# Attention over 512 heads: value loads and stores cut into three partition ranges

## The chip, the cores and the metric

The kernel runs on one core of a Trainium2 chip. The metric is the device time of one execution in microseconds (us); lower is better. Three timed runs of the kernel before took 1209.46, 1211.04 and 1211.22 us, median 1211.04.

The engines are named as in the profile: PE is TensorE (matrix products; PEld is its weight load), DVE is VectorE, ACT is ScalarE, POOL is GpSimd, SP is SyncE, whose queue issues every DMA of this kernel. Sixteen DMA engines carry out the transfers.

## The reference

q has the shape (16, 32, 192, 128), k and v (16, 32, 1024, 128), all in bf16. For each of the 16 x 32 = 512 heads:

```
scale  = 128 ** -0.5
scores = einsum("bhqd,bhkd->bhqk", q, k) * scale
p      = softmax(scores, axis=-1)
out    = einsum("bhqk,bhkd->bhqd", p, v)
```

So 192 queries of a head meet 1024 keys. Keys and values are 134.22 MB each, queries and results 25.17 MB each.

## The kernel before, in words

The 512 heads are worked off in 32 groups of G = 16 heads. Each group has 8 pairs of heads; a pair has 2 x 192 = 384 query rows, cut into three units of 128 rows. So a group has 24 units, and the program 768.

A unit goes through stages that stand some units apart (LAGS): PE multiplies queries and keys into `s_ps` (`qk`); DVE scales, copies to `ss` and takes the extreme value of a row (L335); ACT takes the exponential (L391), or POOL only subtracts the extreme value (L210) and the exponential comes later; PE transposes the 128 x 1024 result in eight pieces (`tr`, into `pt_ps`); ACT copies it to SBUF (L402, L404); PE multiplies it by the values (`pv`, into `o_ps`); DVE divides by the sum of the row and writes `ob` (L362, L365). Where POOL prepared the unit, `pv` also multiplies by a column of ones to get the row sums.

The inputs of a group are double-buffered: `kt`, `qt` and `vs` have NS = 2 slots, and group g uses slot g % 2. `ob` has two slots too (NSO = 2). All transfers are issued by SP, in one order written out by hand:

- At the start the first group comes in three pieces (FIRST, 2, 6 and 8 heads), each with its own semaphores (`sf`, `sfv`); then group 1 in whole by `loads(1)`.
- Then for each group g: `loads(g + 2)`, followed by `stores(g)`.
- `loads(g)` waits until PE has done the last `qk` of group g - 2 (`s_qk`), issues the keys as a DMA transpose (`kt`, L144) and the queries as a DMA transpose (`qt`, L148), waits until PE has done the last `pv` of group g - 2 (`s_pv`), and issues the values as one plain DMA of 4096 KB (`vs`, L155). In the values, partition p holds the keys 8p to 8p + 7 of every head, so one partition of one head is a run of 2 KB.
- `stores(g)` waits for DVE (`s_on`) and writes the group's results as one DMA of 768 KB (L173): 128 partitions with 24 rows of 256 B each. The last group is stored in four pieces (LAST).

Every DMA adds 16 to its semaphore when it has landed, in sixteen steps of one. PE waits for the keys (`sxk`), the queries (`sxq`) and the values (`svl`, L311) of a group at the first unit of that group; the counts come from `load_cnt(g)`, which counts 16 for each earlier use of the slot. DVE waits for the store of group g - 2 before it writes the first pair of group g into the same slot of `ob` (`store_cnt`), and SP waits for all stores at the end.

PE's order in each step is `qk` of the next unit, `pv` of the unit 8 back, `tr` of the unit 4 back; it is one queue in that order, so a wait of one of them holds up the others.

Of the kernel before, what the change touches and what calls it, by code (L numbers as in the profile page):

```python
# [13 lines left out]


def _attention_kernel(nc, q, k, v, out, G=16, NS=2, LAGS=(2, 4, 5, 8), ROUTES=(R_W, R_W, R_EA, R_W, R_EA, R_EA),
                      FIRST=((0, 2), (2, 8), (8, 16)), LAST=((0, 4), (4, 6), (6, 7), (7, 8))):
    B, H, SQ, D = q.shape
    SK = k.shape[2]
    assert D == 128 and SK == 1024 and SQ == 192, (D, SK, SQ)  # L20
# [6 lines left out]
    KT_TILES = SK // 128  # L27
# [7 lines left out]
    NSO = 2  # L35
# [4 lines left out]
    vf = v.rearrange("b h s d -> (b h) s d")  # L40
    of = out.rearrange("b h s d -> (b h) s d")

    def route(u):
        return ROUTES[u % len(ROUTES)]
# [4 lines left out]
    for u in range(NU):  # L49
        r = route(u)  # L50
# [13 lines left out]
    with ExitStack() as es:  # L64
        def sb(name, shape, dt):
            return es.enter_context(nc.sbuf_tensor(name, shape, dt))
# [4 lines left out]
        def sem(name):  # L71
            return es.enter_context(nc.semaphore(name))
# [3 lines left out]
        vs = sb("vs", [128, NS, G, KT_TILES, 128], BF16)  # L76
        ob = sb("ob", [128, NSO, PPG, 3, 128], BF16)
# [14 lines left out]
        svl = [sem("svl%d" % i) for i in range(NS)]  # L92
        sf = [sem("sf%d" % i) for i in range(len(FIRST))]
        sfv = [sem("sfv%d" % i) for i in range(len(FIRST))]
        sst = [sem("sst%d" % i) for i in range(NSO)]
# [13 lines left out]
        def unit_info(u):  # L109
            pr = u // 3  # L110
            k3 = u % 3
            g = pr // PPG
            pg = pr % PPG
            return pr, k3, g, pg
# [6 lines left out]
        def load_cnt(g):  # L121
            return 16 * (g // NS + 1 - (g % NS == 0))

        def store_cnt(g):
            return 16 * (g // NSO + 1)

        def wait_x(eng, u):
            if route(u) == R_W:
# [4 lines left out]
        def wait_evac(eng, u):  # L133
            if route(u) == R_ED:
                eng.wait_ge(s_evd, ev_cnt[u])
            else:
                eng.wait_ge(s_eva, ev_cnt[u])

        @block.sync
        def _(e):  # L140
            def load_kq(g, a, b, sems):
                s = g % NS
                h0 = g * G
                e.dma_start_transpose(  # L144
                    kt[:, s, :, a * 128:b * 128],
                    kf[h0 + a:h0 + b].rearrange("g (p t) d -> (g p) (t d)", t=KT_TILES),
                ).then_inc(sems[0], 16)
                e.dma_start_transpose(  # L148
                    qt[:, s, a * SQ:b * SQ],
                    qf[h0 + a:h0 + b].rearrange("g r d -> (g r) d"),  # L150
                ).then_inc(sems[1], 16)

            def load_v(g, a, b, sm):
                h0 = g * G
                e.dma_start(  # L155
                    vs[:, g % NS, a:b],
                    vf[h0 + a:h0 + b].rearrange("g (p t) d -> p g t d", t=KT_TILES),
                ).then_inc(sm, 16)

            def loads(g):  # L160
                s = g % NS
                last_u = (g - NS + 1) * UPG - 1
                if g >= NS:
                    e.wait_ge(s_qk, last_u + 1)
                load_kq(g, 0, G, (sxk[s], sxq[s]))
                if g >= NS:
                    e.wait_ge(s_pv, last_u + 1)
                load_v(g, 0, G, svl[s])

            def stores(g, a, b):  # L170
                so = g % NSO
                e.wait_ge(s_on, g * PPG + b)
                e.dma_start(  # L173
                    of[g * G + 2 * a:g * G + 2 * b].rearrange("h r d -> (h r) d").rearrange(
                        "(n p) d -> p n d", p=128),
                    ob[:, so, a:b].rearrange("p pg y d -> p (pg y) d"),
                ).then_inc(sst[so], 16)

            n = len(FIRST)
            for i in range(n):  # L180
                load_kq(0, *FIRST[i], (sf[i], sf[i]))
                if i > 0:
                    for i2 in range(i if i > 1 else 0, i + 1):
                        load_v(0, *FIRST[i2], sfv[i2])
            for g in range(1, min(NS, NGR)):
                loads(g)
            for g in range(NGR):
                if g + NS < NGR:
                    loads(g + NS)
                for a, b in (LAST if g == NGR - 1 else ((0, PPG),)):  # L190
                    stores(g, a, b)
            for so in range(min(NSO, NGR)):
                n_uses = len(range(so, NGR, NSO))
                if so == (NGR - 1) % NSO:
                    n_uses += len(LAST) - 1
                e.wait_ge(sst[so], 16 * n_uses)

        @block.gpsimd
        def _(gp):
# [20 lines left out]
        def _(pe):  # L220
            def product(o, w, x, at=(0, 0), start=True, stop=True, transpose=False):

                return pe.add_instruction(mybir.InstMatmult(  # L223
                    name=nc.get_next_instruction_name(),
                    engine=mybir.EngineType.PE,
                    ins=[pe.lower_ap(x), pe.lower_ap(w)],
                    outs=[pe.lower_ap(o)],
                    start_tensor_calc=start,
                    stop_tensor_calc=stop,
                    is_transpose=transpose or None,  # L230
                    tile_size=(128, w.shape[-1]),
                    tile_position=at,
                    bass_skip_group_check=True,
                    ldweights=False,
                ))

            def qk(u):
# [13 lines left out]
                if g == 0:  # L251
                    for i, (h, _) in enumerate(FIRST):
                        if u == 3 * h // 2:
                            pe.wait_ge(sf[i], 32)
                elif u % UPG == 0:
                    pe.wait_ge(sxq[s], load_cnt(g))
# [27 lines left out]
            def pv(u):  # L284
                pr, k3, g, pg = unit_info(u)
                s = g % NS
                O = o_ps[pr % 2]
                PTS = pt_sb[:, u % NPT]
                sl = O_SLOT[k3]
                a = 2 * pg  # L290
                b = 2 * pg + 1
                ins = None
                with_rs = route(u) == R_W
                if k3 < 2:
                    tiles = [((0, 0), slice(0, 128), a if k3 == 0 else b)]
                else:
                    tiles = [((0, 0), slice(0, 64), a), ((0, 64), slice(64, 128), b)]
                wait_evac(pe, u)
                for t in range(KT_TILES):
                    first = t == 0  # L300
                    last = t == KT_TILES - 1
                    for at, rows, x in tiles:
                        w = PTS[:, t, rows]
                        pe.ldweights(w, tile_position=at)  # L304
                        if first and at[1] == 0:
                            if g == 0:
                                for i, (h, _) in enumerate(FIRST):
                                    if u == 3 * h // 2:
                                        pe.wait_ge(sfv[i], 16)
                            elif u % UPG == 0:  # L310
                                pe.wait_ge(svl[s], load_cnt(g))  # L311
                            if k3 == 0 and pr >= 2:
                                pe.wait_ge(s_on, pr - 1)
                        ins = product(O[rows, sl, :], w, vs[:, s, x, t, :], at, first, last)
                        if with_rs:
                            ins = product(O[rows, 3, sl: sl + 1], w, ones[:, 0:1], at, False, last)
                ins.then_inc(s_pv, 1)
# [3 lines left out]
            for step in range(NU + L_PV):  # L321
                if step + 1 < NU:
                    qk(step + 1)
                if 0 <= step - L_PV < NU:
                    pv(step - L_PV)
                if 0 <= step - L_TR < NU:
                    tr(step - L_TR)
# [87 lines left out]
def bass_standalone__mha_softmax__near_ridge_kernel(  # L415
    nc: bass.Bass,
    q: bass.AP,
    k: bass.AP,
    v: bass.AP,
    out: bass.AP,  # L420
):
    _attention_kernel(nc, q, k, v, out)
# [28 lines left out]
```

## Time and profile before

| | before |
|---|---|
| median of 3 timed runs | 1211.04 us |
| the profiled execution's own time | 1208.21 us |
| its span, first to last instruction | 1206.4 us |
| mean granted TensorE clock | 0.993 |
| bytes moved | 321.43 MB, mean 266 GB/s |
| keys: issues, median us from issue to landing | 34, 30.4 |
| queries | 34, 6.3 |
| values, 4096 KB | 31, 15.1 |
| stores, 768 KB | 31, 17.1 |

How to read it: the span is the profiled execution between its first and its last instruction; what lies around it (1208.21 - 1206.4) isn't in the trace. In the DMA view "packets" are single runs of bytes; keys, queries and stores go in packets of 256 B, values in packets of 2 KB, instruction fetches in packets of 16 KB (queue 8) and 8 KB (queue 14). The share of a queue is the time that its packets took against sixteen engines over the span; packets overlap, so it can be over 100%. The time from issue to landing contains the time that a transfer stands behind others, and an issuing instruction on SP can itself take long while the queue is full. A line of waits gives the total in us, the number of waits and the longest one.

### The profile page before, as it was taken

How to read it: one execution, taken by the hardware profiler on the slowest of the kernel's cores; microseconds unless marked ns; L12 is line 12 of the kernel's file. 1: busy time of each engine (PE TensorE's matmuls, PEld its weight loads, DVE VectorE, ACT ScalarE, POOL GpSimd, SP SyncE). 2: the span in 40 equal slices, each digit the busy share in tenths (PEclk: the TensorE clock that was granted, in tenths of full speed). 3: DMA queues.
4: the chain of work that ended last, by engine and by line, in shares of the span. 5: the costliest groups of instructions: out<-in, count | busy, mean ns of one | idle time of the engine just before them, and what ended most of it. 6: DMA issues, size and time to landing. Idle time of an engine off the chain costs nothing.

```text
span 1206.4 us, 41597 instructions
## 1 busy us (share of the span) xinstructions
PE 1165.6 (97%) x19456; PEld 876.5 (73%) x15360; DVE 1077.4 (89%) x2304; ACT 1001.4 (83%) x1537; POOL 722.3 (60%) x390
## 2 busy tenths in 40 slices
PE   4699999999999999999999999999999999999998
PEld 2577777777777777777777777777777777777776
DVE  4589999999989998899999999899999999999996
ACT  3578888888878888888888888888888888888887
POOL 3356656656656665566565656556666666665663
PEclk9899999999999999999999999999999999999999
DMA  9999999999999999999999999999999999999991
GB/s 237 240 285 283 277 282 264 243 297 274 287 268 238 283 282 287 279 239 267 297 283 261 286 257 269 289 271 285 281 259 268 279 290 286 270 234 294 283 268 40
DMA packets 789900, 321.43 MB, mean 266 GB/s; under 512 B 724176, under 2 KB 724176, under 8 KB 789712
## 3 DMA queue, kind: packets, MB, share of 16 engines
q1 hardware_dynamic: 789712, 318.78, 111.8%
q8 instruction: 136, 2.23, 0.7%
q14 instruction: 52, 0.43, 0.1%
HBM read 134.22 MB, written 25.17 MB: 132 GB/s over the span
## 4 chain that ended last, share of the span: by engine, by line
PE 86%; DMA 7%; SPq 5%; issue 1%; DVE 0%; ACT 0%; ACTq 0%; DVEq 0%
PE o_ps L223 31%; PE pt_ps L223 28%; PE s_ps L223 27%; DMA qt<-in_q_dram 7%; SPq L144 5%; DVE ss L335 0%; SPq L148 0%; SPq L155 0%; ACT x_sb L391 0%; ACT pt_sb L402 0%; DVE ob L365 0%; ACT pt_sb L404 0%; DVE rinv L362 0%; ACTq L390 0%; ACTq L400 0%
## 5 line engine op out<-in xcount | busy, mean ns | idle before, releaser
L335 DVE TENSOR_SCALAR_CACHE_REDUCE ss<-s_ps 128x1024 f32<-128x1024 f32 x768 | 914.3, 1219 | 111.7 <-ACT x_sb L391 69.7
L210 POOL TENSOR_TENSOR x_sb<-ss,nb 128x1024 bf16<-128x1024 f32 x384 | 721.6, 1893 | 472.0 <-PE pt_ps L223 461.0
L304 PEld LDWEIGHTS <-pt_sb 128*128 128x128 bf16 (+1 forms) x8192 | 474.6, 103 | 231.2 <-issue 155.7
L223 PE MATMUL o_ps<-vs,pt_sb 128*128 128x128 bf16 (+1 forms) x8192 | 538.6, 218 | 0.0
L223 PE MATMUL s_ps<-kt,qt 128*128 128x512 bf16 (+1 forms) x2048 | 468.2, 388 | 36.7 <-DMA qt<-in_q_dram 35.4
L223 PE MATMUL pt_ps<-ident,x_sb 128*128 128x128 bf16 x6144 | 471.8, 220 | 0.9 <-ACT pt_sb L402 0.8
L402 ACT ACTIVATE pt_sb<-pt_ps 128x1024 bf16<-128x1024 bf16 x384 | 391.1, 1018 | 92.3 <-PE pt_ps L223 92.2
L391 ACT ACTIVATE x_sb<-ss,nb 128x1024 bf16<-128x1024 f32 x384 | 438.4, 1142 | 9.2 <-DVE ss L335 9.2
L278 PEld LDWEIGHTS <-x_sb 128*128 128x128 bf16 x6144 | 354.8, 98 | 26.4 <-issue 2.5
L404 ACT ACTIVATE pt_sb<-pt_ps 128x512 f32<-128x512 f32 x384 | 228.5, 595 | 97.9 <-PE pt_ps L223 97.7
L223 PE MATMUL o_ps<-ones,pt_sb 128*128 128x1 bf16 x3072 | 282.5, 165 | 0.0
L365 DVE TENSOR_TENSOR ob<-o_ps,rinv 128x384 bf16<-128x384 f32 x256 | 142.6, 557 | 8.7
L262 PEld LDWEIGHTS <-qt 128*128 128x128 bf16 (+1 forms) x1024 | 78.8, 102 | 69.0 <-DMA qt<-in_q_dram 31.7
L391 ACT ACTIVATION_READ_ACCUMULATOR x_sb<-ss,nb 128x1 f32 x384 | 74.1, 193 | 0.0
L335 DVE DVE_READ_ACCUMULATOR ss<-s_ps 128x1 f32 x768 | 63.5, 83 | 0.0
L362 DVE RECIPROCAL rinv<-o_ps 128x2 f32<-128x2 f32 (+1 forms) x256 | 42.1, 165 | 6.2 <-PE o_ps L223 6.2
L362 DVE RECIPROCAL rinv<-rs 128x1 f32<-128x1 f32 (+1 forms) x256 | 36.9, 144 | 0.0
L391 ACT ACT_TABLE_LOAD x1 | 1.3, 1283 | 0.8 <-PEq L436 0.8
L200 POOL MEMSET ones<- 128x128 bf16 x1 | 0.2, 204 | 0.3 <-POOLq L436 0.3
L202 POOL TENSOR_SCALAR_AFFINE_SELECT ident<-ones 128x128 bf16<-128x128 bf16 x1 | 0.3, 293 | 0.1
L436 POOL MEMSET const-float32-0.0<- 128x1 f32 x1 | 0.1, 98 | 0.3 <-issue 0.3
L436 POOL MEMSET const-uint8-127<- 128x1 uint8 x1 | 0.1, 102 | 0.0
(2 smaller groups left out, 0.2 us busy)
## 6 DMA issues: line engine op xcount, KB each, us to landing
vs<-in_v_dram SPq DMA_DIRECT2D x31, 4096.0 KB, 15.1
out_dram<-ob SPq DMA_DIRECT2D x31, 768.0 KB, 17.1
vs<-in_v_dram SPq DMA_DIRECT2D x1, 2048.0 KB, 10.3
vs<-in_v_dram SPq DMA_DIRECT2D x1, 1536.0 KB, 8.4
kt<-in_k_dram SPq DMA_TRANSPOSE x34, 30.4
qt<-in_q_dram SPq DMA_TRANSPOSE x34, 6.3
vs<-in_v_dram SPq DMA_DIRECT2D x1, 512.0 KB, 4.8
out_dram<-ob SPq DMA_DIRECT2D x1, 384.0 KB, 3.5
```

The costliest lines, as they stand in the source:

```text
L144: e.dma_start_transpose(kt[:, s, :, a * 128:b * 128], kf[h0 + a:h0 + b].rearrange("g (p t) d -> (g p) (t d)", t=KT_TILES),).then_inc(sems[ ...
L210: gp.tensor_tensor(x_sb[:, u % NX, :], ss[:, u % NSS, :], nb[:, u % NSS: u % NSS + 1].to_broadcast([128, SK]), ALU.subtract,).then_inc(s_x ...
L223: return pe.add_instruction(mybir.InstMatmult(name=nc.get_next_instruction_name(), engine=mybir.EngineType.PE, ins=[pe.lower_ap(x), pe.low ...
L262: pe.ldweights(w, tile_position=at)
L278: pe.ldweights(w, is_transpose=True, tile_position=(0, 0))
L304: pe.ldweights(w, tile_position=at)
L335: dve.tensor_scalar(ss[:, u % NSS, :], s_ps[u % 2][:].rearrange("p t k -> p (t k)"), -scale, None, ALU.mult, ALU.min, accum_out=nb[:, u % ...
L362: dve.reciprocal(rinv[:, pr % 2, sel], src[:, sel]).then_inc(s_ri, 1)
L365: dve.tensor_tensor(ob[:, so, pg], o_ps[pr % 2][:, 0:3, :], rinv[:, pr % 2, 0:3].unsqueeze(2).to_broadcast([128, 3, 128]), ALU.mult,).then ...
L391: act.activation(x_sb[:, u % NX, :], ss[:, u % NSS, :], ACT_FN.Exp, bias=nb[:, u % NSS: u % NSS + 1], scale=-1.0, accum_out=rs[:, pr % NRS ...
L402: act.activation(pt_sb[:, u % NPT], pt_ps[u % 2][:], ACT_FN.Exp, scale=-1.0).then_inc(s_eva, 1)
L404: act.activation(words(pt_sb[:, u % NPT]), words(pt_ps[u % 2][:]), ACT_FN.Copy).then_inc(s_eva, 1)
```

## The change

The values of a group are loaded by four DMAs in place of one: heads 0 to 5 of the group with all 128 partitions (V_EVEN = 6), and heads 6 to 15 in three DMAs for the partitions 0-111, 112-119 and 120-127 (V_PARTS). Each store becomes three DMAs for the partitions 0-111, 112-123 and 124-127 (STORE_PARTS), in the last group for each of its four pieces. The waits count accordingly: PE waits for 4 x 16 for each use of a slot of `vs`, DVE and the end of the program for 3 x 16 for each store. The first group's values (FIRST) stay as they are, and so do keys, queries and all that the engines compute. The same bytes move.

```diff
-                      FIRST=((0, 2), (2, 8), (8, 16)), LAST=((0, 4), (4, 6), (6, 7), (7, 8))):
+                      FIRST=((0, 2), (2, 8), (8, 16)), LAST=((0, 4), (4, 6), (6, 7), (7, 8)),
+                      STORE_PARTS=((0, 112), (112, 124), (124, 128)), V_EVEN=6, V_PARTS=((0, 112), (112, 120), (120, 128))):
...
         def store_cnt(g):
-            return 16 * (g // NSO + 1)
+            return 16 * len(STORE_PARTS) * (g // NSO + 1)
...
-            def load_v(g, a, b, sm):
+            def load_v(g, a, b, sm, parts=((0, 128),)):
                 h0 = g * G
-                e.dma_start(
-                    vs[:, g % NS, a:b],
-                    vf[h0 + a:h0 + b].rearrange("g (p t) d -> p g t d", t=KT_TILES),
-                ).then_inc(sm, 16)
+                for lo, hi in parts:
+                    e.dma_start(
+                        vs[lo:hi, g % NS, a:b],
+                        vf[h0 + a:h0 + b].rearrange("g (p t) d -> p g t d", t=KT_TILES)[lo:hi],
+                    ).then_inc(sm, 16)
...
-                load_v(g, 0, G, svl[s])
+                load_v(g, 0, V_EVEN, svl[s])
+                load_v(g, V_EVEN, G, svl[s], V_PARTS)
...
                 e.wait_ge(s_on, g * PPG + b)
-                e.dma_start(
-                    of[g * G + 2 * a:g * G + 2 * b].rearrange("h r d -> (h r) d").rearrange(
-                        "(n p) d -> p n d", p=128),
-                    ob[:, so, a:b].rearrange("p pg y d -> p (pg y) d"),
-                ).then_inc(sst[so], 16)
+                rows = of[g * G + 2 * a:g * G + 2 * b].rearrange("h r d -> (h r) d").rearrange(
+                    "(n p) d -> p n d", p=128)
+                for lo, hi in STORE_PARTS:
+                    e.dma_start(
+                        rows[lo:hi],
+                        ob[lo:hi, so, a:b].rearrange("p pg y d -> p (pg y) d"),
+                    ).then_inc(sst[so], 16)
...
-                e.wait_ge(sst[so], 16 * n_uses)
+                e.wait_ge(sst[so], 16 * len(STORE_PARTS) * n_uses)
...
-                                pe.wait_ge(svl[s], load_cnt(g))
+                                pe.wait_ge(svl[s], (1 + len(V_PARTS)) * load_cnt(g))
```

## The prediction

> **What bounds the kernel now.** First the page: engines, DMA queues, and the chain that ended last.
>
> ```profile
> PE 1165.6 (97%) x19456; PEld 876.5 (73%) x15360; DVE 1077.4 (89%) x2304; ACT 1001.4 (83%) x1537; POOL 722.3 (60%) x390
> ...
> q1 hardware_dynamic: 789712, 318.78, 111.8%
> q8 instruction: 136, 2.23, 0.7%
> ...
> PE 86%; DMA 7%; SPq 5%; issue 1%; DVE 0%; ACT 0%; ACTq 0%; DVEq 0%
> ```
>
> TensorE looks like the bound, but the chain also passes through the landing of the next group's queries, and the queue of kernel DMAs is full all the time. Beside it runs a small queue of 136 instruction fetches of 16 KB, one every 8.5 us. Next, TensorE's waits from 60 to 1160 us, that is, without the start and the end:
>
> ```profile
> PE s_ps L223 <- DMA qt<-in_q_dram: 20.5, 13, 8.7
> ```
>
> In 13 groups TensorE starts late because the transposed queries are late. The timeline gives the price: where it doesn't wait, the first score product of one group starts 36.02 us after that of the one before (573.52 to 609.55 us); from group 1 (59.78 us) to group 31 (1158.24 us) the mean is 36.62. So 30 groups lose 0.60 us each, 17.9 us in all. That is the most that better transfers can bring.
>
> Now the SyncE queue, one group of its timeline:
>
> ```profile
> 317.58 28.01 SPq L144 DMA_TRANSPOSE kt<-in_k_dram  x1
> 345.62 4.17 SPq L148 DMA_TRANSPOSE qt<-in_q_dram  x1
> 349.84 0.58 SPq L155 DMA_DIRECT2D vs<-in_v_dram  x1
> 350.47 4.11 SPq L173 DMA_DIRECT2D out_dram<-ob  x1
> 354.62 28.12 SPq L144 DMA_TRANSPOSE kt<-in_k_dram  x1
> ```
>
> It has no gap, and the order of transfers is always keys, queries, values, store. Last, the DMA view of five stretches: values (97 to 103 us), store (142.5 to 144), the end of a store (106.5 to 108.5), keys undisturbed (109 to 112), keys beside an instruction fetch (112.5 to 114).
>
> ```profile
> DMA packets 1155, 2.37 MB, mean 394 GB/s; under 512 B 0, under 2 KB 0, under 8 KB 1155
> ...
> DMA packets 1653, 0.44 MB, mean 294 GB/s; under 512 B 1643, under 2 KB 1643, under 8 KB 1653
> ...
> DMA packets 965, 0.24 MB, mean 122 GB/s; under 512 B 965, under 2 KB 965, under 8 KB 965
> ...
> DMA packets 3397, 0.87 MB, mean 290 GB/s; under 512 B 3397, under 2 KB 3397, under 8 KB 3397
> ...
> DMA packets 142, 0.04 MB, mean 24 GB/s; under 512 B 142, under 2 KB 142, under 8 KB 142
> ```
>
> Two things lose time. During the transposes one 16 KB fetch, a single packet and so the work of one DMA engine, brings all sixteen nearly to a halt (24 instead of 290 GB/s for 1.5 us): the transposes go in step. During values and store the engines run free, and then the next transposes wait for the last of them (122 instead of 290 GB/s for 2 us). The landing records show who is late: every DMA adds one to its semaphore for each of its sixteen shares, and over the first 29 stores the middle share lands 0.27 us after the first one, the last share 1.86 us after the first one. So some engine is 1.6 us behind the middle when keys should start. At the 290 GB/s of undisturbed keys, the 4 us after a store's first share lose 1.22 us on average. The change works on this loss alone; the halts inside the transposes stay.
>
> **The change, part by part.** The sum is made against the profiled execution: span 1206.4, its own time 1208.21 us, 2.8 under the median of 1211.04. I apply the difference to the median.
>
> 1. Packets per engine. Before, each engine has 8 partitions: 8 x 16 = 128 value packets of 2 KB and 8 x 24 = 192 store packets of 256 B per group. After, I take 112 partitions as sixteen shares of 7, and 8, 12 and 4 partitions as one each on the lowest 8, 12 and 4 engines; the change's description says which way it goes, and no row shows it. Values: six heads stay at 8 x 6 = 48 packets; of ten heads the engines 0 to 7 get 9 x 10 = 90, the others 70. Totals 138 and 118. Stores: 9 x 24 = 216 on engines 0 to 3, 192 on 4 to 11, 168 on 12 to 15.
> A value packet costs 6000 x 16 / 1155 = 83 ns, a store packet 1500 x 16 / 1653 = 14.5 ns. So engines 0 to 3 get 10 x 83 + 24 x 14.5 = 1.18 us more, engines 12 to 15 get 1.18 us less, 4 to 7 get 0.83 more, 8 to 11 get 0.83 less.
> 2. What the keys wait for. If the late engine is among 12 to 15, it falls from 1.59 us behind the middle (1.86 - 0.27) to 0.4, and the last ones are now engines 0 to 3, at 1.18 plus a scatter of some 0.1 to 0.2: about 1.3. Gain 0.3 us a group, 30 x 0.3 = 9 us. Ends: at best the whole 17.9 us of TensorE's waits go and TensorE alone sets the period; at worst the late engine is one of 0 to 3 and everything is 1.18 later, +35 us. I take 0.3 as nearest to the landing records.
> 3. Queue work on SyncE. Three more value loads at 0.58 us and two more stores at 0.37 us (the shortest store issue, on an empty queue): 3 x 0.58 + 2 x 0.37 = 2.5 us per group, 75 us in all if bare. I cost it at nothing: keys are issued about 10 us before their packets move (96.59 us, while the store ahead of them lands at 106.5 to 108.6), and the added issues eat 2.5 of that. The first value load still goes out straight after the queries.
> 4. Waits. PE waits for 4 x 16 counts of values in place of 16, DVE for 3 x 16 of the store, the end of the program likewise. Behind PE's value wait stand that group's weighted sums and all later products. Values land 13.2 us after the queries (365.1 against 351.9 us for group 9), and the wait comes 14.6 us after the group's first score product (366.7 against 352.05): cover 1.4 us. It holds if values land no later than now, as in step 2. DVE's wait on the store of two groups before has some 3 us.
> 5. The end. The last store becomes three issues: 2 x 0.4 = +0.8 us, bare.
> 6. Partial shapes. Every plain transfer of the trace before covers 128 partitions, so how fast ten packets to one partition go is not shown. Lower end: the 83 ns of the free run, nothing added. Upper: packets of engines that get in each other's way; the nearest row is the first 3 us of a value load, 322 GB/s (92.9 to 96 us), 102 ns a packet, 20 x 19 ns = 0.4 us more on engines 0 to 7; the far end is a four times longer packet, set by the 24 to 122 GB/s that rows with waiting engines show, 20 x 83 x 3 = 5.0 us. I take the lower end, since the free run is most of the load, and keep the others as a rival.
>
> Sum: -9 + 0.8 = -8 us: 1211.0 - 8 = **1203**.
>
> [...]
>
> **Rivals.**
> - *The small loads crowd (slower).* For: nothing of that shape in the trace; and the margin is thin, since step 2 gains only while the twenty extra-part packets take less than 0.3 us more together, 15 ns each. Against: in the free run packets go at a steady 83 ns. At twice the packet time: engines 0 to 7 at 1.3 + 20 x 83 ns = 3.0 us behind, 1.4 more than the 1.59 now, x 30 = +42, time 1254. At four times: 1.3 + 5.0 - 1.6 = 4.7, x 30 = +141, time 1352; values would then land after TensorE's wait for them too, at no further cost beyond the same delay.
> - *The late engine is one of the low ones (slower).* For: the records don't name it. Against: only the description. +35 and 0.8: 1247.
> - *No shift, or the lag only changes places (same).* If the added load equals what the late engine loses, or the shares fall otherwise than in step 1: 1211 + 0.8, 1209 to 1213.
> - *More is regained (faster).* If keys start as early as the middle engine, DMA falls under 36.02 us a group: 1211.0 - 17.9 + 0.8 = 1194.
>
> **How the numbers follow.** A measurement of this kernel can tell 0.2% (2.4 us) from no change. Faster as in the sum, 1193 to 1208, with 1194 as its best end: 0.50. No shift: 0.10. Late low engine: 0.07. Crowding: 0.33, of which some 0.14 lies below 1275. The likeliest is 1203; its own range is 1193 to 1208. The range up to 1275 holds 0.50 + 0.10 + 0.07 + 0.14 = 0.81.
>
> **What would show it.** Right: the mean period of groups 1 to 31 at 36.2 to 36.4 us; TensorE's wait for the queries in mid-run at 8 to 14 us instead of 20.5; after a store the last share within 1.4 us of the middle; the value stretch still near 390 GB/s. Wrong by crowding: value loads that land at 15 us or more after the queries, a rate well under 390 GB/s before their end, and new waits of PE at the weighted sums. Wrong on step 3: keys' packets that start with a gap after the store, with the SyncE issue close ahead of them. Wrong on the engine: the last share later by about 1.2 us, values at full rate.

## The result and the profile after

The changed kernel takes 1413.31 us (median of 4 runs, 1410.09 to 1423.51) against 1210.28 for the kernel before: a ratio of 1.171, 95% interval 1.166 to 1.175 (the two medians alone give 1.168). The forecast was 1203, range up to 1275. The profiled execution took 1410.09 us, its span is 1408.3.

The page of the changed kernel, in the order shown for before: engines, DMA queues, the chain by engine and by line.

```profile
PE 1229.7 (87%) x19456; PEld 918.7 (65%) x15360; DVE 1081.1 (77%) x2304; ACT 1005.4 (71%) x1537; POOL 722.2 (51%) x390
...
q1 hardware_dynamic: 791264, 318.79, 107.4%
q8 instruction: 136, 2.23, 0.7%
...
PE 43%; DMA 38%; SPq 18%; issue 1%; ACT 0%; DVE 0%; ACTq 0%
DMA vs<-in_v_dram 38%; PE o_ps L228 16%; PE pt_ps L228 14%; PE s_ps L228 13%; SPq L157 9%; SPq L149 5%; SPq L145 4%; ACT x_sb L396 0%; ACT pt_sb L407 0%; ACT pt_sb L409 0%; DVE ob L370 0%; DVE rinv L367 0%; ACTq L395 0%
```

The same bytes move, and the chain now runs through the landing of the values for 38% of the span. TensorE's waits from 60 to 1360 us say the same (total, number, longest):

```profile
PE o_ps L228 <- DMA vs<-in_v_dram: 135.9, 30, 6.3
PE s_ps L228 <- DMA qt<-in_q_dram: 10.4, 11, 1.5
```

In every one of 30 groups the weighted sums wait for values, 4.5 us on average, a wait that wasn't there before; the wait for queries fell from 20.5 to 10.4 us, as TensorE now comes later itself. One group on SyncE's queue:

```profile
331.60 16.91 SPq L145 DMA_TRANSPOSE kt<-in_k_dram  x1
348.55 4.49 SPq L149 DMA_TRANSPOSE qt<-in_q_dram  x1
353.08 4.72 SPq L157 DMA_DIRECT2D vs<-in_v_dram  x4
357.85 18.54 SPq L179 DMA_DIRECT2D out_dram<-ob  x3
376.44 17.52 SPq L145 DMA_TRANSPOSE kt<-in_k_dram  x1
```

The issue of the stores now holds the queue for 18.5 us. But the keys' packets start at 379.8 us, when the last share of the store lands, and their issue began 3.4 us earlier (2.2 to 3.6 us over 25 groups in mid-run): the queue is held by full transfers, it doesn't hold them. TensorE and VectorE don't hold it either: over the same groups the keys were issued 18 us or more after the last score product that they wait for, and the stores 27 us or more after the results that they wait for. Where the time goes is in the DMA view of four stretches of that group: six heads over 128 partitions (357 to 359.9), ten heads over 112 (360.2 to 368), the small loads with store packets beside them (370 to 373.5, 917 of 1022 packets under 512 B), the rest of the store (374 to 379.5).

```profile
DMA packets 574, 1.15 MB, mean 398 GB/s; under 512 B 11, under 2 KB 11, under 8 KB 574
...
DMA packets 938, 1.93 MB, mean 247 GB/s; under 512 B 4, under 2 KB 4, under 8 KB 937
...
DMA packets 1022, 0.44 MB, mean 127 GB/s; under 512 B 917, under 2 KB 917, under 8 KB 1022
...
DMA packets 2262, 0.60 MB, mean 109 GB/s; under 512 B 2257, under 2 KB 2257, under 8 KB 2260
```

Whole-partition values still go at 398 GB/s. At the border to the 112-partition load the rate drops to 247: 7800 x 16 / 938 = 133 ns a packet against 83. The records of landing (last share of each transfer, mean of groups 4 to 28) give the same by stage; "in" is the time at which the last share has landed:

| us per group | before | after |
|---|---|---|
| queries in to values in | 12.58 | 19.22 |
| values in to store in | 2.69 | 3.26 |
| store in to next keys in | 18.18 | 17.78 |
| keys in to queries in | 3.27 | 3.13 |
| sum | 36.72 | 43.38 |

Of the 6.66 us a group, 6.64 are values, 0.57 stores; the transposes gave 0.5 back. The mean period of TensorE from group 1 to 31 went from 36.62 to 43.12 us; 30 x 6.5 = 195 of the 202 us by which the span grew.

The records also bear on step 1 of the prediction: a group leaves 50 of them for its four value loads and 34 for its three store parts. That fits 16 + 16 + 9 + 9 and 16 + 13 + 5, that is, sixteen shares for a 112-partition part and 8, 8, 12 and 4 for the small ones, each with one record more that makes up the count of 16. So the number of engines is as step 1 took it; which engines they are isn't shown.

### The profile page after: what moved, and what is told of

The parts are those of the page before. It is cut to its first block, busy times and chain, and to the rows that moved or that the text cites. A ratio compares the mean times of both kernels' runs of the same rounds, so it can differ in the third digit from the quotient of the medians.

```text
span 1408.3 us, 41760 instructions
## 1 busy us (share of the span) xinstructions
PE 1229.7 (87%) x19456; PEld 918.7 (65%) x15360; DVE 1081.1 (77%) x2304; ACT 1005.4 (71%) x1537; POOL 722.2 (51%) x390
## 4 chain that ended last, share of the span: by engine, by line
PE 43%; DMA 38%; SPq 18%; issue 1%; ACT 0%; DVE 0%; ACTq 0%
DMA vs<-in_v_dram 38%; PE o_ps L228 16%; PE pt_ps L228 14%; PE s_ps L228 13%; SPq L157 9%; SPq L149 5%; SPq L145 4%; ACT x_sb L396 0%; ACT pt_sb L407 0%; ACT pt_sb L409 0%; DVE ob L370 0%; DVE rinv L367 0%; ACTq L395 0%
## 5 line engine op out<-in xcount | busy, mean ns | idle before, releaser
L309 PEld LDWEIGHTS <-pt_sb 128*128 128x128 bf16 (+1 forms) x8192 | 496.2, 106 | 392.3 <-issue 319.4
L228 PE MATMUL o_ps<-vs,pt_sb 128*128 128x128 bf16 (+1 forms) x8192 | 561.9, 221 | 140.8 <-DMA vs<-in_v_dram 140.8
L228 PE MATMUL s_ps<-kt,qt 128*128 128x512 bf16 (+1 forms) x2048 | 486.1, 400 | 33.5 <-DMA qt<-in_q_dram 32.4
L228 PE MATMUL pt_ps<-ident,x_sb 128*128 128x128 bf16 x6144 | 492.7, 226 | 0.9 <-ACT pt_sb L407 0.8
L283 PEld LDWEIGHTS <-x_sb 128*128 128x128 bf16 x6144 | 373.8, 101 | 26.5 <-issue 2.6
L228 PE MATMUL o_ps<-ones,pt_sb 128*128 128x1 bf16 x3072 | 304.1, 171 | 0.0
```

The source lines that it names most:

```text
L228: return pe.add_instruction(mybir.InstMatmult(name=nc.get_next_instruction_name(), engine=mybir.EngineType.PE, ins=[pe.lower_ap(x), pe.low ...
L283: pe.ldweights(w, is_transpose=True, tile_position=(0, 0))
```

## The experiments

The theories. A, crowding: over a range of neighbouring partitions other than all 128, packets take longer, as the 133 ns of the 112-partition load against 83 suggest; why they would, no run shows. B: each added DMA costs by itself. C: only the shifted load counts, as in steps 1 and 2. Ratios are to the kernel before on the same chip, which took 1202.6 to 1204.6 us in these experiments, while the expectations count from 1211; a difference in us is to the former.

**Stores alone, values alone.** On the changed kernel, one half undone each. For the stores alone the values are whole again, and PE's wait counts 16 again:

```diff
-load_v(g, 0, V_EVEN, svl[s])
-load_v(g, V_EVEN, G, svl[s], V_PARTS)
+load_v(g, 0, G, svl[s])
```

> [...] Theory B (the number of DMAs: each added issue costs): two of the five added DMAs, so two fifths of the 203 us, about 1290. Theory C (only the uneven load of the engines counts): four engines with 0.36 us more, at most 1222.

For the values alone the stores are whole again:

```diff
-STORE_PARTS=((0, 112), (112, 124), (124, 128))
+STORE_PARTS=((0, 128),)
```

> Theory A: nearly the whole loss, 1360 to 1400 us, with value packets of 126 to 164 ns in the 112-partition part and over 230 ns in the small ones. Theory B: three of the five added DMAs, about 1330. Theory C: engines 0 to 7 have 0.83 us more, at most 1236.

Measured: stores alone 1.009 (1.008 to 1.011), 11 us; values alone 1.152 (1.150 to 1.154), 183 us. The values are nine tenths of the loss. The values alone fell in A's range (1360 to 1400), far from B and C. For the stores B's number missed by far, while C's bound of 1222 holds at 1215; the stage values-in to store-in grew 0.49 us, so slower packets may be there too, by little. Whether A, C or the two added DMAs (see the next run) cost these 11 us isn't shown.

**As many DMAs, whole partitions.** On the kernel before:

```diff
-load_v(g, 0, G, svl[s])
+for a, b in ((0, 6), (6, 10), (10, 13), (13, 16)):
+    load_v(g, a, b, svl[s])
...
+for c, d in ((0, 3), (3, 6), (6, 8)):     # in place of one store of 8 pairs
+    store(g, c, d)
```

> As many DMAs as in the changed kernel, but each over all 128 partitions: values as four loads of 6, 4, 3 and 3 heads, each store as three of 3, 3 and 2 pairs. Theory A and theory C: as before, 1211 within 5 us. Theory B: as the changed kernel, about 1410.

Measured: 1.018 (1.014 to 1.022), 20 us. No theory said so: A and C expected no change, B the whole loss. B is out as the main cause, but the number of DMAs isn't free: by the landing records 0.64 us a group, spread over values (+0.26), store (+0.15), keys (+0.05) and queries (+0.2).

**Even load, uneven shape.** On the values-alone run:

```diff
-V_PARTS=((0, 112), (112, 120), (120, 128))
+V_PARTS=((0, 112), (112, 128))
```

> Values of ten heads as 112 and 16 partitions, so seven and one for each of sixteen engines, all engines loaded alike; stores whole. Theory A: as slow as with 112, 8 and 8 or a little less, 1330 to 1400 us, since 112 partitions are crowded already and sixteen neighbouring ones too. Theory B: two added DMAs, about 1290. Theory C: even load, 1211.

```diff
-V_PARTS=((0, 112), (112, 120), (120, 128))
+V_PARTS=((0, 64), (64, 128))
```

> Values of ten heads as two loads of 64 partitions, stores whole; four partitions of each load for each of sixteen engines, an even load. [...]

Measured: 1.134 (1.132 to 1.137) and 1.145 (1.142 to 1.148), 1364.38 and 1376.82 us; the first is in A's range, and the second lost no less. In both, every engine has as many packets as before (each part leaves 16 records of landing). So C can't be the loss; B's 1290 for two more DMAs is out as well. Two halves of 64 partitions show the slower packets most plainly: first six heads over 128 partitions (518.5 to 522 us), then 64 partitions each (524 to 528 and 530.5 to 534).

```profile
DMA packets 568, 1.18 MB, mean 337 GB/s; under 512 B 2, under 2 KB 2, under 8 KB 566
...
DMA packets 416, 0.84 MB, mean 210 GB/s; under 512 B 6, under 2 KB 6, under 8 KB 416
...
DMA packets 421, 0.73 MB, mean 208 GB/s; under 512 B 82, under 2 KB 82, under 8 KB 420
```

4000 x 16 / 416 = 154 ns a packet, nearly twice the 83 ns of the free run: sixteen engines write 64 partitions at 210 and 208 GB/s here, against 337 GB/s in the same trace's stretch of whole partitions, and against 394 and 398 in the free runs of the kernels before and after.

**The 112-partition load alone.** As values alone, but the two small loads are left out from group 2 on, so 16 partitions of ten heads keep old data:

```diff
-V_PARTS=((0, 112), (112, 120), (120, 128))
+V_PARTS=((0, 112),)
```

> Values of ten heads over partitions 0 to 111 only (partitions 112 to 127 of them are left out from group 2 on), stores whole: the 112-partition shape without the small loads. If the small loads alone crowd, as the prediction's rival had it: no loss, 1195 to 1211. If the 112-partition load itself crowds: its 70 packets at about 145 ns take 10 us in place of 5.8, so 4 us a group, about 1300 to 1330.

Measured: 1.065 (1.062 to 1.067), 78 us. The stretch inside that load (531.5 to 537.5 us):

```profile
DMA packets 790, 1.54 MB, mean 257 GB/s; under 512 B 56, under 2 KB 56, under 8 KB 787
```

6000 x 16 / 787 = 122 ns a packet, although fewer bytes move. So the large part, which my prediction costed at nothing, costs 78 us here, less than expected (1281.75 us against 1300 to 1330). The small loads put back bring the 183 us of the values-alone run, 105 more. The landing records split it in the same way: values are in 12.6 us after the queries before, 15.4 us with the 112-partition load alone, 19.1 us with the small loads put back.

**Near or apart.** The cleanest pair. On the kernel before, one more load a group into a buffer that nobody reads: eight heads of eight partitions, once four apart, once side by side. The number of engines (9 records of landing for each load in both, so eight), packets, bytes and DMAs are alike. The kernel waits for each of these loads before it issues the next. Four apart:

```diff
+e.dma_start(scr[0:32:4], vf[g * G:g * G + 8].rearrange("g (p t) d -> p g t d", t=KT_TILES)[0:32:4])
```

> The kernel before, with one more load per group, into a buffer that nobody reads: 8 heads of the partitions 0, 4, 8 ... 28, that is eight packets of 2 KB for eight engines. It adds 8 x 83 ns = 0.66 us to engines 0 to 7 and nothing to the late engine, if that is a high one. Late engine high, as the prediction took it: hidden under its lag of 1.6 us, 1211 within 5 us. Late engine among 0 to 7: 30 x 0.66 = 20 us, about 1231. Theory B (a DMA more costs by itself): a fifth of 203 us, about 1250.

Side by side:

```diff
+e.dma_start(scr[112:120], vf[g * G:g * G + 8].rearrange("g (p t) d -> p g t d", t=KT_TILES)[112:120])
```

> The same extra load of the same size, on as many engines, but of the neighbouring partitions 112 to 119. [...] Theory B and C: the same as the run with partitions apart.

Measured: apart 1209.18 us, 1.005 (1.003 to 1.007), 6.6 us and so a little more than the 5 us given; side by side 1253.54 us, 1.042 (1.040 to 1.044). The difference is 44 us, 1.4 us for each of 31 loads. It has the direction of theory A; B and C said none. One thing isn't separated here: the rows read from HBM change together with the partitions written (8 KB apart in one run, one 16 KB run of each head in the other), in this pair as in every other run, and the two also lie at other places (0 to 28 and 112 to 119). So it is shown that the load of neighbouring partitions costs 1.4 us more than that of partitions apart, and in the traces above that packets over 112 and over 64 partitions take 122 to 154 ns in place of 83; what holds them up, no run shows. TensorE's waits show the same over the whole run; apart, then side by side:

```profile
PE s_ps L232 <- DMA qt<-in_q_dram: 36.0, 15, 8.5
```

```profile
PE s_ps L232 <- DMA qt<-in_q_dram: 52.1, 24, 8.8
PE o_ps L232 <- DMA vs<-in_v_dram: 11.2, 13, 1.6
```

**Is the late engine a high one?** One whole head in place of that load, so the same eight packets on all sixteen engines:

```diff
+e.dma_start(scr[:], vf[g * G].rearrange("(p t) d -> p t d", t=KT_TILES))
```

> The kernel before with one more load per group into a buffer that nobody reads: one head over all 128 partitions, so eight packets for each of the sixteen engines, among them the late one. The run with partitions apart put the same eight packets on engines 0 to 7 alone and cost 6.6 us. If the late engine is among 8 to 15, as the prediction took it, its 8 x 83 ns = 0.66 us now come on top: 30 x 0.66 = 20 us over before, about 1223, some 13 us more than the run with partitions apart. If the late engine is among 0 to 7, both cost the same, about 1209.

Measured: 1.0165 (1.0146 to 1.0184). That is 1.15%, 14 us, more than the same packets on eight engines alone (13 were expected). That fits slack in the engines of the small load that the others lack. Steps 1 and 2 took the late engine for a high one, outside the eight; this speaks for it, but the run also moves twice the bytes, and no record names the engines.

**Values on ScalarE's queue.** To see whether the transfers of a group set the period, and for a better version, the values of groups 2 to 31 went to ScalarE:

```diff
+act.wait_ge(s_pv, (g - NS + 1) * UPG)
+act.dma_start(vs[:, g % NS], vf[g * G:(g + 1) * G]...).then_inc(svl[g % NS], 16)
...
+g = (step - L_PV - 2) // UPG + NS - 1
+if (step - L_PV - 2) % UPG == 0 and NS <= g < NGR: load_v(g)
```

> The kernel before with the values of groups 2 to 31 issued by ScalarE, once the weighted sums that free the slot are done, instead of by SyncE behind the queries. If the two queues of an engine take turns, value packets fill the halts of the transposes beside an instruction fetch (some 1.3 us each), the transfers of a group fall under TensorE's 36.02 us and up to 18 us go: 1185 to 1200. If the transposes in step are slowed by values between them, queries land later: 1205 to 1240.

Measured: 1.018 (1.017 to 1.020), 1225.81 us, in the second range. Queries took 18.2 us from issue to landing instead of 6.3, with values beside them. Then the same with 14 and with 17 in place of L_PV + 2 = 10 units:

> As the run with values on ScalarE's queue, but issued four units (6 us) later, when the keys of the group are nearly in. There the queries took 18 us from issue to landing, because values went beside them, and were late in most groups. If only that collision cost the time, queries now land some 29 us after the keys' start and TensorE never waits: 1186 to 1200. If the transfers still need more than 36.02 us a group in sum: 1203 to 1225.

> The same, seven units (10.5 us) later than at first, when the queries are in and the queue of SyncE holds only the store. If only the collision of values and queries cost the time: 1186 to 1200, and the keys of the next group run beside the end of the values. If keys in step are slowed by values beside them, or the transfers need more than 36.02 us a group: 1203 to 1225.

Measured: 0.998 (0.997 to 0.999) and 0.996 (0.994 to 0.998), medians 1202.25 and 1201.73 us, just under the second range and above the first. With 17 the twelve executions spread from 1191.77 to 1214.49 us: two took 1191.77 and 1192.92, and the ratio leaves out three over 1210; what made the two fast is not known, as the trace kept is of one of 1211.02 us. The first of the two runs waits like this from 60 to 1160 us:

```profile
PE s_ps L222 <- DMA qt<-in_q_dram: 8.2, 1, 8.2
```

There, from group 3 on every period (from a group's first score product to the next group's) is 36.03 us, with queries in some 8 to 14 us early: the bound of the transfers is gone. But at group 2 values and queries still meet, once, and what was won is lost there (that period is 46.70 us). Two attempts to move ScalarE's part away from that place:

```diff
-if (step - 14) % UPG == 0 and NS <= g < NGR:     # ScalarE's values: from group 2 on
+if (step - 14) % UPG == 0 and NS < g < NGR:      # from group 3 on; SyncE loads the rest
```

> Values on ScalarE's queue as in the run with four units more, but from group 3 on only; the values of group 2 go by SyncE behind the queries, as before, since in that run they met the queries of group 2 and cost TensorE about 10 us there, once. Expected: periods of 36.03 us from group 2 to 31 and 10 to 15 us less than before, 1186 to 1196. If the collision only moves to group 3: 1200 to 1204.

```diff
-g = (step - 14) // UPG + NS - 1
-if (step - 14) % UPG == 0 and NS < g < NGR:
-    load_v(g)
+V_STEPS = {(g - NS + 1) * UPG + {3: 20, 4: 18}.get(g, 15): g for g in range(NS + 1, NGR)}
+if step in V_STEPS:
+    load_v(V_STEPS[step])
```

> As the run with ScalarE's queue from group 3 on, with the values of groups 3 and 4 issued six and four units later and all others one unit later, so that they find the queries of their group in. There the one collision cost TensorE some 10 us at groups 2 to 4, and all later periods were 36.03 us. Without it: 1186 to 1196. If another collision takes its place: 1200 to 1206.

Measured: 1.000 (0.998 to 1.001) and 1.001 (1.000 to 1.003). Each time the collision came one group later (periods of 43.16 and 46.12 us). Both times fell in the range given for a collision that moves. So by its ratio none of these is more than half a per cent faster than before, and only the two above are faster at all.

**How the loss acts.** On a kernel whose queries are early, added transfer time should be hidden. First five more DMAs as in the equal-number run, on the run with ScalarE's values from group 3 on (1202.87 us):

> The same kernel with five more DMAs per group over all 128 partitions (values as 6, 4, 3 and 3 heads, stores as 3, 3 and 2 pairs). In the kernel before these cost 20 us (0.64 us a group). If they cost time because the transfers of a group set the period: hidden here by queries that land 8 to 13 us early, within 4 us of the run without them. If each DMA costs somewhere else (the end, SyncE's order, TensorE's waits): again about 20 us more.

Measured: 1.040 (1.037 to 1.042), 1250.45 us, which neither number said. It doesn't answer the question about the transfers: ScalarE's queue was held up to 5.0 us by an issue, and TensorE waited for ScalarE.

```profile
PE pt_ps L235 <- ACT pt_sb L414: 43.5, 27, 7.5
```

Then the change's stores, on SyncE's queue, on top of the run with groups 3 and 4 later:

```diff
+for lo, hi in ((0, 112), (112, 124), (124, 128)):
+    e.dma_start(rows[lo:hi], ob[lo:hi, so, a:b]...).then_inc(sst[so], 16)
```

> The same with the change's stores in three partition ranges, which cost 11 us on the kernel before. If that cost acts through the sum of a group's transfers against TensorE's 36.02 us, it is hidden here by queries that land early: within 3 us of the run without it. If it acts in another way (through DVE's wait for the store, or the end): again about 11 us more.

Measured: 1203.18 us against 1204.75 without them. Each of the two loses time in the first groups alone; from group 6 on every period is 36.03 us in both. The 11 us of the split stores are gone, so they act through the sum of a group's transfers against TensorE's period, not each by itself. For the values, which are most of the loss, this wasn't tried.

## Why the prediction was wrong, point by point

- **Step 6 failed**, and with it the whole. It looked only at the small loads (twenty packets on eight engines) and took the lower end, 83 ns. The 112-partition load was counted as seven free packets per head and engine; it measured 133 ns, so 70 x 50 ns = 3.5 us a group there alone, where the prediction had nothing. The small loads weren't free either: put back, they land the values 3.7 us a group later (15.4 to 19.1 us after the queries), where 20 packets at 83 ns take 1.7. No row of the trace before has such a shape; I leaned on "the free run is most of the load", but the free run was that of 128 partitions. The rival "the small loads crowd" had the slower packets, at a third of the chance, with one term missing: 1254 to 1352 us against 1413. Its signs came: values 19.2 us after the queries, 247 GB/s before their end, new waits at the weighted sums.
- **Steps 1 and 2** aren't refuted. Eight extra packets on eight engines cost 6.6 us, on all sixteen 14 us more. What the late engine lost is invisible under 6.6 us a group of slower transfers, so the 9 us gain was never tested.
- **Step 3**: the cover shrank from about 10 us to 2.2 to 3.6 us and held. But the term "at nothing" was mis-sized: five more DMAs over whole partitions cost 20 us (0.64 us a group). They do so through the stages of the transfers and not through SyncE, which still issued the keys 2.5 us or more before the store ahead of them was in.
- **Step 4**: the cover for the values was about right. The weighted sums of group 9 start at 367.5 us and not 366.7, and over 25 groups they start 1.8 us on average (0.7 to 2.6) after the values are in, against the 1.4 us read. Its condition, that values land no later than now, is what failed: they land 19.2 us after the queries while before their wait came 14 to 15 us after the first score product, and TensorE waits 4.5 us a group.
- **Step 5** (0.8 us at the end) fits, as far as one trace each can tell: from the first score product of the last group to the end the stores-alone run took 48.9 us, the kernel before 48.2.
- The bound was read rightly: 36.02 us a group is TensorE's own period; with values on ScalarE's queue it was reached (36.03) from group 3 on.

## What to carry to other kernels

Before packets are balanced among DMA engines by partition ranges, check what a partial range does to the time of one packet (here 122 to 154 ns in place of 83), with one extra load into an unused buffer, side by side against apart. When an edit cuts a large transfer into a large and some small parts, the large part has a new shape too, and is to be priced first. Here, where transfers and the busiest engine were level (36.6 against 36.0 us), added transfer time came out nearly in full: 6.5 of 6.7 us a group.

## What the runs showed of the hardware that was not expected

- Eight partitions side by side against eight partitions four apart: the same bytes and DMAs, 44 us apart in time.
- Two 64-partition loads run at 208 to 210 GB/s and 112 partitions at 247 to 257, where whole partitions reach 394 to 398.
- Five more whole-partition DMAs a group cost 0.64 us a group.
- In the changed kernel, where TensorE waits in every group, the granted clock was lower: 0.933 against 0.993 before, and the key products took 400 ns on average in place of 388. By the table of stages the transfers set the period, so this should not be part of the loss; no run tested it.
